# Attention and three-way maxout on one core: a fourth sum bank, reordered sums and splits, and pairs of batches run to and fro

## The chip, the core and the metric

The kernel runs on one core of a Trainium2 chip. A core has a matrix engine (TensorE, in the profile PE, with its weight loads as PEld), VectorE (DVE), ScalarE (ACT), GpSimd (POOL) and a queue that issues transfers (SyncE, SP). Matrix products go into PSUM, eight banks of 512 fp32 columns per partition; VectorE and ScalarE read them from there; everything else lies in SBUF or, through transfers, in HBM. The metric is the device time of one execution in microseconds (us), as the median of several runs. Lower is better.

## The reference

```python
scores = scale * np.matmul(q, k.transpose(0, 1, 3, 2)) - np.log(S)
attn = 1.0 / (1.0 + np.exp(-scores))
x = np.matmul(attn, v)                 # then laid out as (B * S, H * D)
h = np.maximum(np.maximum(x @ w1, x @ w2), x @ w3)
return (h @ w_out).astype(np.float32)
```

There are 8 batches, 12 heads, 448 positions and 64 columns a head, so `x` is 3584 x 768, and the four weights are 768 x 768. The weights reach the kernel as 64-bit numbers, and it turns them into fp32 itself.

## The kernel before

It has two phases. **Attention** runs 24 rounds (8 batches by 3 groups of four heads). A round computes scores (line L267, and the last 64 positions of both pairs of heads at L279), has ACT take the sigmoid (L258), and multiplies by v (L287, L296); the sums are copied out of PSUM by VectorE (L316) and stored to `x_dram`. In the background, two blocks a round, raw weights are decoded (two operations on ACT, L173 and L174, four on VectorE, L175 to L184). The generator `decoding` holds their order `todo`: the 12 blocks of stage 0 stay in SBUF, the 36 of later stages are stored to `w_dram` and fetched back when needed.

**Products** computes all four matrix products in 4 stages: stages 0 to 2 give one third of the rows of `h` each and take the maximum over the three weights (q = 0, 1, 2); stage 3 is the product with `w_out`, where q counts thirds of the output's rows. A stage visits 4 pairs of batches, so there are 16 visits (numbered 0 to 15 here), each with three passes q. A visit multiplies 2 x 2 blocks by a scheme with 7 block products instead of 8: `PRODUCTS` lists which sum of weight blocks meets which sum of x blocks, and which PSUM bank takes the result. The sums of blocks are made by POOL, for x (`x_load`, L231, four subtractions of 128x1344) and for weights (`w_combine`, L134). Each operand is split into a high part (a cast on ACT, L361 for x, L145 for weights) and the rest (a subtraction on VectorE, L362 for x, L146 for weights), and a product is three terms over three k-blocks: 9 matmuls of 448 columns (L370).

After product k, VectorE and ACT read the banks. With p1 = the first product, copied by ACT (L426): `u2` = second + p1 (L429), `u3` = second + fourth + p1 (L432), and four results m22, m11, m21, m12 are put together by `put` (L403 for a first or only value, L405, L408 and L409 where a maximum is taken). For stages 0 to 2 the results go to `h_dram`, for stage 3 to the output.

Every engine runs its instructions in the order in which the code records them (`pin`), and a transfer waits in SP's queue behind those recorded before. At the start of a visit the next visit's x blocks are fetched (`x_load`), and during q = 2 they are split, one name after each product. Weights of the next stage are fetched and split around the last visit and the first visit of a stage (`w_load`, `w_split`): q = 0's in the last visit, q = 1's and q = 2's in the first. The blocks of x, their parts and the weights' parts have one buffer each, so a fetch waits until the former content has been read.

Of the kernel before, what the change touches and what calls it, by code (L numbers as in the profile page):

```python
# [38 lines left out]
def attention_then_maxout(  # L39
# [58 lines left out]
    m_p = pool(ctx, "m", 1)  # L98
    ps_av = pool(ctx, "ps_av", 1, space=PSUM)
# [48 lines left out]
    def decoding(dec_p):  # L148
# [64 lines left out]


    def x_load(src, p):


        r = {}
        for row in range(2):
            for th in range(2):  # L220
                name = f"b{row + 1}{th + 1}"
                r[name] = xs_p.tile([P, HALF, S], F32, name=f"xs_{name}")
                t = (2 * p + th) * S
                pin(nc.sync.dma_start(out=r[name], in_=src[row][:, :, t : t + S]))
# [3 lines left out]
        for out, in0, in1 in (  # L228
            ("t1", "b12", "b11"), ("t2", "b22", "t1"), ("t3", "b22", "b12"), ("t4", "b21", "t2"),
        ):  # L230
            pin(nc.gpsimd.tensor_tensor(out=r[out], in0=r[in0], in1=r[in1], op=ALU.subtract))  # L231
        return r


    def attention(stack):
# [68 lines left out]
        def load(n):  # L304
            if n < len(fours):
                b, f = fours[n]
                first = load_qk(b, 2 * f)
                vt = load_v(b, f)
                loads[n] = (first, load_qk(b, 2 * f + 1)), vt

        def finish(n, pss):
# [10 lines left out]
        before = xs = None  # L322
# [169 lines left out]
```

## Time and profile before

| | us |
|---|---|
| median of 3 runs | 1003.41 (1002.44 to 1004.03) |
| the profiled execution | 1008.24 |
| its span, first to last instruction | 1006.5 |
| PE busy | 924.3 (92% of the span) |
| VectorE busy | 599.9 |
| ScalarE busy | 413.9 |
| GpSimd busy | 257.4 |
| attention, up to the first product | 292.97 |

A busy share is a mean over phases: ScalarE is busy 205 of the first 293 us and little later. Matmuls overlap each other, so PE's busy time counts short waits only in part; a stretch of matmuls, from start to start, tells more.

### The profile page before, as it was taken

How to read it: one execution, taken by the hardware profiler on the slowest of the kernel's cores; microseconds unless marked ns; L12 is line 12 of the kernel's file. 1: busy time of each engine (PE TensorE's matmuls, PEld its weight loads, DVE VectorE, ACT ScalarE, POOL GpSimd, SP SyncE). 2: the span in 40 equal slices, each digit the busy share in tenths (PEclk: the TensorE clock that was granted, in tenths of full speed). 3: DMA queues.
4: the chain of work that ended last, by engine and by line, in shares of the span. 5: the costliest groups of instructions: out<-in, count | busy, mean ns of one | idle time of the engine just before them, and what ended most of it. 6: DMA issues, size and time to landing. Idle time of an engine off the chain costs nothing.

```text
span 1006.5 us, 12056 instructions
## 1 busy us (share of the span) xinstructions
PE 924.3 (92%) x4560; PEld 684.5 (68%) x4560; DVE 599.9 (60%) x794; ACT 413.9 (41%) x513; POOL 257.4 (26%) x116
## 2 busy tenths in 40 slices
PE   6999998999989999978799998879999969799998
PEld 2333333333348898867789897768889858699997
DVE  2656745644463765848884673888575658656262
ACT  5777676776770421414241330415042223324130
POOL 0110102200004044062604225351404352431400
PEclk9999999999998999999799999889999979899999
DMA  5767778777842304131412404140330514252421
GB/s 206 231 233 238 264 259 314 267 270 243 272 150 66 123 24 147 45 141 61 141 40 107 147 19 159 50 160 19 128 113 34 178 32 174 78 183 80 177 74 74
DMA packets 74043, 143.93 MB, mean 143 GB/s; under 512 B 6400, under 2 KB 58624, under 8 KB 73984
## 3 DMA queue, kind: packets, MB, share of 16 engines
q1 hardware_dynamic: 73984, 143.16, 41.4%
q8 instruction: 36, 0.59, 0.2%
q14 instruction: 23, 0.19, 0.1%
HBM read 103.02 MB, written 40.11 MB: 142 GB/s over the span
## 4 chain that ended last, share of the span: by engine, by line
PE 57%; DVE 25%; DMA 6%; issue 6%; ACT 3%; POOL 2%; SPq 1%; DVEq 0%; ACTq 0%; POOLq 0%
PE ps_y L370 35%; PE ps_av L287 9%; PE ps_s L267 9%; DVE xlo_t L362 8%; DVE xlo_b L362 5%; DMA xs_b<-x_dram 2%; DVE c L408 2%; PE ps_av L296 2%; DVE wlo_a L146 2%; DMA xs_b<-h_dram 2%; DVE u L429 2%; PE ps_s L279 1%; ACT a L258 1%; DVE wlo_s L146 1%; DMA qk<-qk 1%
## 5 line engine op out<-in xcount | busy, mean ns | idle before, releaser
L370 PE MATMUL ps_y<-xhi_t,wlo_s 128*128 128x448 f32 x432 | 165.0, 382 | 43.3 <-DVE u L429 43.3
L231 POOL TENSOR_TENSOR xs_t<-xs_b,xs_b 128x1344 f32<-128x1344 f32 x16 | 49.6, 3103 | 558.6 <-DMA xs_b<-x_dram 435.2
L258 ACT ACTIVATE a<-ps_s,bias_s 128x896 f32<-128x896 f32 x168 | 158.2, 1005 | 83.5 <-PE ps_s L279 44.6
L370 PE MATMUL ps_y<-xhi_t,whi_s 128*128 128x448 f32 x432 | 161.9, 375 | 0.0
L370 PE MATMUL ps_y<-xlo_t,whi_s 128*128 128x448 f32 x432 | 161.8, 375 | 0.1
L267 PE MATMUL ps_s<-qk 64*128 64x448 f32 x576 | 125.2, 568 | 11.5 <-DMA qk<-qk 8.2
L370 PEld LDWEIGHTS ps_y<-xhi_t,wlo_s 128*128 128x128 f32 x432 | 83.2, 193 | 62.0 <-DVE u L429 49.1
L287 PE MATMUL ps_av<-a,v 128*64 128x448 f32 x576 | 119.9, 552 | 2.6 <-DVE m L316 2.6
L426 ACT COPY p<-ps_y 128x448 f32<-128x448 f32 x48 | 25.6, 533 | 230.5 <-PE ps_y L370 227.7
L267 PEld LDWEIGHTS ps_s<-qk 64*128 64x128 f32 x576 | 52.8, 190 | 81.1 <-issue 55.0
L370 PE MATMUL ps_y<-xhi_b,wlo_a 128*128 128x448 f32 x288 | 107.6, 373 | 0.0
L183 DVE CUSTOM_DVE_ANT_0 wb<-wraw,wb 128x768 uint16<-128x768 uint16 x48 | 32.9, 685 | 124.9 <-ACT wraw L174 124.1
L370 PE MATMUL ps_y<-xlo_b,whi_a 128*128 128x448 f32 x288 | 106.9, 371 | 0.0
L370 PE MATMUL ps_y<-xhi_b,whi_a 128*128 128x448 f32 x288 | 106.4, 369 | 0.0
L231 POOL TENSOR_TENSOR xs_t<-xs_b,xs_t 128x1344 f32<-128x1344 f32 x32 | 100.3, 3135 | 9.6 <-DMA xs_b<-x_dram 7.6
L362 DVE TENSOR_TENSOR xlo_b<-xs_b,xhi_b 128x1344 fp32r<-128x1344 f32 x48 | 76.3, 1589 | 36.5 <-PE ps_y L370 19.8
L287 PEld LDWEIGHTS ps_av<-a,v 128*64 128x64 f32 x576 | 37.5, 138 | 80.8 <-issue 62.3
L370 PEld LDWEIGHTS ps_y<-xhi_t,whi_s 128*128 128x128 f32 x432 | 83.8, 194 | 7.2
L370 PEld LDWEIGHTS ps_y<-xlo_t,whi_s 128*128 128x128 f32 x432 | 83.5, 193 | 6.9 <-DVE xlo_t L362 0.5
L401 ACT COPY m<-ps_y 128x448 f32<-128x448 f32 x24 | 12.8, 533 | 160.8 <-PE ps_y L370 160.8
L362 DVE TENSOR_TENSOR xlo_t<-xs_t,xhi_t 128x1344 fp32r<-128x1344 f32 x48 | 75.6, 1601 | 0.0
L370 PE MATMUL ps_y<-xhi_t,wlo_a 128*128 128x448 f32 x144 | 55.3, 384 | 21.2 <-DVE u L432 21.2
(58 smaller groups left out, 1449.4 us busy)
## 6 DMA issues: line engine op xcount, KB each, us to landing
xs_b<-x_dram SPq DMA_DIRECT2D x48, 672.0 KB, 6.7
qk<-qk SPq DMA_DIRECT2D x48, 448.0 KB, 4.5
wraw<-w SPq DMA_DIRECT2D x36, 384.0 KB, 6.2
v<-v SPq DMA_DIRECT2D x24, 448.0 KB, 3.4
x_dram<-m SPq DMA_DIRECT2D x48, 224.0 KB, 6.1
h_dram<-m SPq DMA_DIRECT2D x48, 224.0 KB, 1.9
xs_b<-h_dram SPq DMA_DIRECT2D x16, 672.0 KB, 7.5
outT<-m SPq DMA_DIRECT2D x48, 224.0 KB, 1.9
```

What stands on the lines that cost most here:

```text
L146: pin(nc.vector.tensor_tensor(out=lo, in0=r[name], in1=hi.bitcast(F32), op=ALU.subtract))
L183: pin(nc.vector.tensor_tensor(out=bits, in0=bits, in1=low, op=ALU.add))
L231: pin(nc.gpsimd.tensor_tensor(out=r[out], in0=r[in0], in1=r[in1], op=ALU.subtract))
L258: pin(nc.scalar.activation(out=a, in_=ps[:, :, :S], func=AF.Sigmoid, bias=bias_s, scale=scale))
L267: pin(nc.tensor.matmul(ps[:, e, :S], t[r, S + c * P : S + (c + 1) * P], t[r, :S], start=True, stop=True,))
L287: pin(nc.tensor.matmul(ps[e * D : (e + 1) * D, :S], vt[:, (g * C + c) * 2 + e], a[:, e], start=c == 0, stop=False,))
L296: pin(nc.tensor.matmul(ps[e * D : (e + 1) * D, :S], vt[r, 4 * C + e], a[r, e], start=False, stop=True,))
L362: pin(nc.vector.tensor_tensor(out=lo, in0=r[name], in1=hi.bitcast(F32), op=ALU.subtract))
L370: pin(nc.tensor.matmul(ps[:, :S], wt[:, k * P : (k + 1) * P], xt[:, k], start=first and n == 0, stop=n == len(terms) - 1, skip_group_check ...
L408: pin(nc.vector.tensor_tensor(out=c, in0=y, in1=add, op=ALU.add))
L426: pin(nc.scalar.copy(out=p1, in_=ps[0][:, :S]))
L429: pin(nc.vector.tensor_tensor(out=u2, in0=ps[1][:, :S], in1=p1, op=ALU.add))
```

## The change

The fourth product of `PRODUCTS` (s3 with t3) becomes the third and gets a bank of its own, and `u3` is now made from that bank and `u2`. The result m21 adds `u3` to a product that stands alone. Banks 0 and 1 keep two buffers, 2 and 3 have one, and line numbers move (products now L389, `u2` L481, `u3` L484, x splits L250, weight splits L148).

```diff
 PRODUCTS = (
     ("a11", "b11", 0),
     ("s2", "t2", 1),
+    ("s3", "t3", 3),
     ("s1", "t1", 2),
-    ("s3", "t3", 1),
...
-                first = ps[bank] is None
+                here = n, q, k
+                first = k < 4 or bank == 1
                 if first:
-                    ps[bank] = ps_y.tile([P, 512], F32, name=f"ps_y{bank}")
+                    ps[bank] = ps_y.tile(
+                        [P, 512], F32, name=f"ps_y{bank}", bufs=2 if bank < 2 else 1
+                    )
...
+                elif k == 2:
+                    u3 = c_p.tile([P, S], F32, name="u3", bufs=1)
+                    pin(nc.vector.tensor_tensor(out=u3, in0=ps[3][:, :S], in1=u2, op=ALU.add))
                 elif k == 3:
-                    u3 = c_p.tile([P, S], F32, name="u3", bufs=1)
-                    pin(nc.vector.tensor_tensor(out=u3, in0=ps[1][:, :S], in1=p1, op=ALU.add))
                     put("22", ps[2], u3)
...
-                    put("21", ps[1], p1)
+                    put("21", ps[1], u3)
```

Casts and splits are set by tables: after product k of pass q of visit n, `his` names an x cast, `los` an x split, `ws` weight splits, `w_loads` a fetch of weights. Stage 1 visits the pairs backwards, so the x of visit 3 serves visit 4, and that of visit 7 visit 8.

```diff
+    visits = [(st, p) for st in range(STAGES) for p in (pairs[::-1] if st == 1 else pairs)]
...
+    for n in range(1, done):
+        (st0, p0), (st, p) = visits[n - 1], visits[n]
+        if st != st0:
+            if st < LAST:
+                when = [[(n - 1, 1, k // 2) for k in range(7)],
+                        [(n - 1, 2, 2 + k // 2) for k in range(7)],
+                        [(n, 0, 3 + k // 2) for k in range(6)] + [(n, 1, 0)]]
+            else:
+                when = [[(n - 1, 1, k // 2) for k in range(7)],
+                        [(n - 1, 2, 5)] * 2 + [(n, 0, 1)] * 2 + [(n, 0, 4)] * 2 + [(n, 0, 5)],
+                        [(n, 1, 3 + k // 2) for k in range(7)]]
...
+            w_loads[n - 2, 0, 0] = st, 0
+            w_loads[when[0][-1]] = st, 1
+            w_loads[when[1][-1]] = st, 2
+        if (st == LAST, p) != (st0 == LAST, p0):
+            for k, (_, name, _) in enumerate(PRODUCTS):
+                his[n - 1, 2, k] = name
+            keys = [(n - 1, 2, k) for k in range(1, 5)] + [(n, 0, k) for k in (0, 2, 3)]
+            for key, (_, name, _) in zip(keys, PRODUCTS):
+                los[key] = name
...
+    for _, name, _ in PRODUCTS[2:4]:
+        x_lo(*x_hi(name, xs))
+    for k in (1, 2, 3):
+        his[0, 0, k - 1] = los[0, 0, k] = PRODUCTS[k + 3][1]
```

In attention, the first call of the generator only issues loads; 8 blocks of later stages follow each 4 of stage 0, and one weight split of stage 0 goes behind each; the buffer `wd` of a decoded block is single; q and k are loaded ahead of v; the first pair is fetched in 12 pieces, one a round from round 10 on, instead of 4 blocks in round 12; the first two x operands are cast and split while the last matmuls of attention run (their pool `xo` now lies beside attention's).

```diff
-            todo += first[4 * q : 4 * q + 4] + later[2 * q : 2 * q + 2]
-        todo += later[6:]
+            todo += first[4 * q : 4 * q + 4] + later[8 * q : 8 * q + 8]
+        todo += later[24:]
...
+            if k == 0:
+                yield
...
-                out = dec_p.tile([P, HP], F32, name="wd", bufs=2)
+                out = dec_p.tile([P, HP], F32, name="wd", bufs=1)
                 decode(raws[k], out)
                 pin(nc.sync.dma_start(out=w_dram[st, q][:, n], in_=out))
-                if ready and k > 16:
-                    for name, _, _ in PRODUCTS:
-                        w_split(ready[0], name, ready[1], nc.vector.tensor_copy)
-                    ready = None
+                if splits:
+                    w_split(*splits.pop(0), nc.vector.tensor_copy)
...
+            else:
+                for _, name, _ in PRODUCTS[:2]:
+                    x_lo(*x_hi(name, xs))
...
-            if n == len(fours) // 2:
-                xs = x_load(x_dram, 0)
+            part = n - 10
+            if 0 <= part < 4 * HALF:
+                x_block(xs, x_dram, 0, part // HALF // 2, part // HALF % 2, part % HALF)
+                if part == 4 * HALF - 1:
+                    x_combine(xs)
```

Three places in the order of instructions carry the prediction. The first is VectorE's queue around the end of visit 0 and the start of visit 1, from m11 of q = 2 to the first results of q = 0 (`xlo` are splits, `u2`, `u3`, `m` and `c` the sums). Before:

```order
L405 TENSOR_TENSOR m11_2512<-ps_y0_2618,m11_2512 128x448
L362 TENSOR_TENSOR xlo_b21_2695<-xs_b21_2445,xhi_b21_2694 128x1344
L408 TENSOR_TENSOR c_2707<-ps_y1_2634,p1_2628 128x448
L409 TENSOR_TENSOR m21_2523<-c_2707,m21_2523 128x448
L362 TENSOR_TENSOR xlo_t4_2712<-xs_t4_2451,xhi_t4_2711 128x1344
L408 TENSOR_TENSOR c_2724<-ps_y2_2650,u2_2644 128x448
L409 TENSOR_TENSOR m12_2534<-c_2724,m12_2534 128x448
L362 TENSOR_TENSOR xlo_b22_2729<-xs_b22_2447,xhi_b22_2728 128x1344
L429 TENSOR_TENSOR u2_2769<-ps_y1_2759,p1_2757 128x448
L432 TENSOR_TENSOR u3_2790<-ps_y1_2759,p1_2757 128x448
```

The same stretch after the change:

```order
L454 TENSOR_TENSOR m11_2518<-ps_y0_2633,m11_2518 128x448
L250 TENSOR_TENSOR xlo_t1_2695<-xs_t1_2442,xhi_t1_2694 128x1344
L457 TENSOR_TENSOR c_2723<-ps_y1_2713,u3_2674 128x448
L458 TENSOR_TENSOR m21_2536<-c_2723,m21_2536 128x448
L457 TENSOR_TENSOR c_2739<-ps_y2_2680,u2_2658 128x448
L458 TENSOR_TENSOR m12_2547<-c_2739,m12_2547 128x448
L250 TENSOR_TENSOR xlo_b21_2710<-xs_b21_2438,xhi_b21_2709 128x1344
L481 TENSOR_TENSOR u2_2784<-ps_y1_2774,p1_2771 128x448
L484 TENSOR_TENSOR u3_2796<-ps_y3_2786,u2_2784 128x448
L250 TENSOR_TENSOR xlo_t4_2728<-xs_t4_2444,xhi_t4_2727 128x1344
L452 TENSOR_TENSOR m22_2809<-ps_y2_2799,u3_2796 128x448
L250 TENSOR_TENSOR xlo_b22_2744<-xs_b22_2440,xhi_b22_2743 128x1344
```

Three splits (b21, t4, b22) have moved from between the last sums of q = 2 into q = 0 of the next visit, each behind that product's sum.

The second place is VectorE's queue from the last decoded block of attention on. Before:

```order
L184 SCALAR_TENSOR_TENSOR wd_2365<-wa_2366,wb_2367 128x384
L362 TENSOR_TENSOR xlo_b11_2408<-xs_b11_1371,xhi_b11_2407 128x1344
L362 TENSOR_TENSOR xlo_t2_2412<-xs_t2_1380,xhi_t2_2411 128x1344
L316 COPY m11_2415<-ps_av0_2375 128x448
L316 COPY m12_2418<-ps_av1_2376 128x448
L362 TENSOR_TENSOR xlo_t1_2422<-xs_t1_1379,xhi_t1_2421 128x1344
L362 TENSOR_TENSOR xlo_t3_2426<-xs_b12_1373,xhi_t3_2425 128x1344
L362 TENSOR_TENSOR xlo_b21_2430<-xs_b21_1375,xhi_b21_2429 128x1344
L362 TENSOR_TENSOR xlo_t4_2434<-xs_t4_1381,xhi_t4_2433 128x1344
L362 TENSOR_TENSOR xlo_b22_2438<-xs_b22_1377,xhi_b22_2437 128x1344
L429 TENSOR_TENSOR u2_2478<-ps_y1_2468,p1_2466 128x448
```

After the change:

```order
L250 TENSOR_TENSOR xlo_t2_2399<-xs_t2_2210,xhi_t2_2398 128x1344
L250 TENSOR_TENSOR xlo_t3_2427<-xs_b12_1441,xhi_t3_2426 128x1344
L250 TENSOR_TENSOR xlo_t1_2431<-xs_t1_2209,xhi_t1_2430 128x1344
L481 TENSOR_TENSOR u2_2474<-ps_y1_2464,p1_2459 128x448
L250 TENSOR_TENSOR xlo_b21_2462<-xs_b21_1742,xhi_b21_2461 128x1344
L484 TENSOR_TENSOR u3_2490<-ps_y3_2480,u2_2474 128x448
L250 TENSOR_TENSOR xlo_t4_2477<-xs_t4_2211,xhi_t4_2476 128x1344
L452 TENSOR_TENSOR m22_2506<-ps_y2_2496,u3_2490 128x448
L250 TENSOR_TENSOR xlo_b22_2493<-xs_b22_2023,xhi_b22_2492 128x1344
L334 COPY c_2520<-ps_av0_2386 128x448
L334 COPY c_2523<-ps_av1_2387 128x448
```

`u2` now stands behind four splits instead of seven and two copies; the copies are behind the third result.

The third place is POOL's queue in visits 11 and 12 of the changed kernel, where stage 3 begins (`xs` sums belong to x, `ws` to weights):

```order
L231 TENSOR_TENSOR xs_t4_5913<-xs_b21_5907,xs_t2_5912 128x1344
L136 TENSOR_TENSOR ws_s1_6088<-ws_a21_6082,ws_a22_6083 128x384
L136 TENSOR_TENSOR ws_s2_6089<-ws_s1_6088,ws_a11_6080 128x384
L136 TENSOR_TENSOR ws_a21_6082<-ws_a11_6080,ws_a21_6082 128x384
L136 TENSOR_TENSOR ws_s4_6090<-ws_a12_6081,ws_s2_6089 128x384
L231 TENSOR_TENSOR xs_t1_6259<-xs_b12_6253,xs_b11_6251 128x1344
L231 TENSOR_TENSOR xs_t2_6260<-xs_b22_6257,xs_t1_6259 128x1344
L231 TENSOR_TENSOR xs_b12_6253<-xs_b22_6257,xs_b12_6253 128x1344
L231 TENSOR_TENSOR xs_t4_6261<-xs_b21_6255,xs_t2_6260 128x1344
L136 TENSOR_TENSOR ws_s1_6371<-ws_a21_6365,ws_a22_6366 128x384
L136 TENSOR_TENSOR ws_s2_6372<-ws_s1_6371,ws_a11_6363 128x384
```

and in the kernel before, at the same place:

```order
L231 TENSOR_TENSOR xs_t4_5910<-xs_b21_5904,xs_t2_5909 128x1344
L134 TENSOR_TENSOR ws_s1_5923<-ws_a21_5917,ws_a22_5918 128x384
L134 TENSOR_TENSOR ws_s2_5924<-ws_s1_5923,ws_a11_5915 128x384
L134 TENSOR_TENSOR ws_a21_5917<-ws_a11_5915,ws_a21_5917 128x384
L134 TENSOR_TENSOR ws_s4_5925<-ws_a12_5916,ws_s2_5924 128x384
L134 TENSOR_TENSOR ws_s1_6128<-ws_a21_6122,ws_a22_6123 128x384
L134 TENSOR_TENSOR ws_s2_6129<-ws_s1_6128,ws_a11_6120 128x384
```

The sums for q = 0 of stage 3 are gone from this place (they are made in visit 10 now); those for q = 2 stay behind the pair's subtractions in both.

More of the change, by code (lines that the diff above doesn't have):

```diff
@@ L98, in attention_then_maxout @@
     m_p = pool(ctx, "m", 1)
+    xo_p = [pool(ctx, "xo", 1)]
     ps_av = pool(ctx, "ps_av", 1, space=PSUM)
@@ L187, in decode @@
             ))
-        stage, ready = None, None
+        stage, splits = None, []
         for k, (st, q, n) in enumerate(todo):
@@ L202, in decoding, with x_block, x_combine @@
                     w_combine(stage)
-                    ready = q, stage
+                    splits = [(q, name, stage) for name, _, _ in PRODUCTS]
             else:
-                out = dec_p.tile([P, HP], F32, name="wd", bufs=2)
+                out = dec_p.tile([P, HP], F32, name="wd", bufs=1)
                 decode(raws[k], out)
                 pin(nc.sync.dma_start(out=w_dram[st, q][:, n], in_=out))
-                if ready and k > 16:
-                    for name, _, _ in PRODUCTS:
-                        w_split(ready[0], name, ready[1], nc.vector.tensor_copy)
-                    ready = None
+                if splits:
+                    w_split(*splits.pop(0), nc.vector.tensor_copy)
             yield
[L215 to L224, printed above, removed]
+        assert not splits
+    def x_block(r, src, p, row, th, k=None):
+        name = f"b{row + 1}{th + 1}"
+        if name not in r:
+            r[name] = xs_p.tile([P, HALF, S], F32, name=f"xs_{name}")
+        ks = slice(0, HALF) if k is None else slice(k, k + 1)
+        t = (2 * p + th) * S
+        pin(nc.sync.dma_start(out=r[name][:, ks], in_=src[row][:, ks, t : t + S]))
+    def x_combine(r):
         for name in ("t1", "t2", "t4"):
@@ L231, in x_load, with x_hi, x_lo @@
             pin(nc.gpsimd.tensor_tensor(out=r[out], in0=r[in0], in1=r[in1], op=ALU.subtract))
-        return r
+    def x_load(src, p):
+        r = {}
+        for row in range(2):
+            for th in range(2):
+                x_block(r, src, p, row, th)
+        x_combine(r)
+        return r
+    FIRST = [x for _, x, _ in PRODUCTS[:2]]
+    def x_hi(name, r):
+        hi = xo_p[name not in FIRST].tile([P, HALF, S], F32R, name=f"xhi_{name}")
+        lo = xo_p[name not in FIRST].tile([P, HALF, S], F32R, name=f"xlo_{name}")
+        pin(nc.scalar.copy(out=hi, in_=r[name]))
+        return name, r[name], hi, lo
+    def x_lo(name, x, hi, lo):
+        pin(nc.vector.tensor_tensor(out=lo, in0=x, in1=hi.bitcast(F32), op=ALU.subtract))
+        x_ops[name] = hi, lo
     def attention(stack):
@@ L306, in load, with finish @@
                 b, f = fours[n]
[L307 to L311, printed above, removed]
+                ts = load_qk(b, 2 * f), load_qk(b, 2 * f + 1)
+                loads[n] = ts, load_v(b, f)
+        def finish(n, pss, pool=m_p, names=("m11", "m12")):
             b, f = fours[n]
@@ L321, in attention @@
         load(0)
-        before = xs = None
+        before, xs = None, {}
         for n in range(len(fours) + 1):
```

74 lines of the change are left out of this document (33 added, 41 removed).

## The prediction

> **What bounds the kernel now.** I start with the chain of work that ended last, by engine, to see which engine sets the end.
>
> ```profile
> PE 57%; DVE 25%; DMA 6%; issue 6%; ACT 3%; POOL 2%; SPq 1%; DVEq 0%; ACTq 0%; POOLq 0%
> ```
>
> PE carries the chain, and VectorE a quarter of it: PE has too much to do to be fed late, and VectorE feeds it late. To see where, I cut the busy time of the product line (L370) into stretches: attention, visit 0, visits 1 and 2, then by turns the two visits around a change of stage and two quiet ones, at last visits 13 and 14, and visit 15. The columns are the stretch, its length, PE's busy time (matmuls), the granted clock, the DMA share and GB/s.
>
> ```profile
> 0.00:292.97 292.97, 0.00 (x1) 0.99 0.73 248
> 292.97:339.47 46.50, 41.53 (x189) 0.93 0.24 75
> 339.47:420.04 80.57, 77.68 (x379) 1.00 0.26 92
> 420.04:521.21 101.17, 84.93 (x379) 0.92 0.28 96
> 521.21:601.77 80.56, 77.70 (x379) 1.00 0.26 92
> 601.77:701.98 100.21, 84.44 (x379) 0.91 0.28 97
> 701.98:782.94 80.96, 78.41 (x379) 1.00 0.26 91
> 782.94:886.68 103.74, 85.16 (x380) 0.90 0.33 114
> 886.68:964.55 77.87, 77.14 (x380) 1.00 0.40 142
> 964.55:1006.47 41.92, 38.46 (x190) 1.00 0.21 78
> 886.68:912.21 25.53, 25.53 (x127) 1.00 0.51 182
> ```
>
> The last row is a stretch without a wait: 14 products (126 matmuls) in 25.53 us, so a product takes 1.824 us and a visit of 21 at least 38.3 us. That is the floor that this change can't lower. Each stretch minus its floor is what the change can win: 8.2 us in visit 0; 4.0, 4.0 and 4.4 in the three quiet pairs (12.3); 24.6, 23.6 and 27.1 around the changes of stage (75.4); 1.3 in visits 13 and 14. Visit 15 has 3.6 us, the drain of the last block, which both kernels have.
>
> What ends a wait in a quiet visit is seen in VectorE's and PE's rows in order of time (start, length, operation; in brackets the idle time before it and who ended it):
>
> ```profile
> 344.05 1.55 DVE L362 TENSOR_TENSOR xlo_b<-xs_b,xhi_b 128x1344 fp32r<-128x1344 f32 x1
> 345.52 0.62 DVE L429 TENSOR_TENSOR u<-ps_y,p 128x448 f32<-128x448 f32 x1
> ...
> 346.20 0.47 PE L370 MATMUL ps_y<-xhi_t,wlo_s 128*128 128x448 f32 x1 [1.10 <-DVE u L429]
> ```
>
> The product s3·t3 wants the bank that `u2` is still to read, and `u2` stands behind a split.
>
> In attention the length of a round (from one L279 to the next) shows the losses; the fifth stretch belongs to a later argument:
>
> ```profile
> 8.76:25.34 16.58, 13.35 (x66) 4.46 (x68) 5.65 (x12) 10.35 (x15) 0.00 (x0) 0.90 0.44 168
> 25.34:36.73 11.39, 11.39 (x69) 4.21 (x65) 5.67 (x10) 8.38 (x11) 4.17 (x4) 1.00 0.70 232
> 48.12:60.45 12.33, 11.46 (x69) 4.21 (x64) 8.06 (x18) 8.48 (x11) 0.00 (x0) 1.00 0.64 215
> 164.84:181.59 16.75, 13.10 (x68) 4.78 (x64) 12.99 (x10) 8.59 (x11) 11.50 (x4) 0.90 0.89 337
> 479.20:482.50 3.30, 3.30 (x11) 2.92 (x10) 0.59 (x2) 0.00 (x0) 0.00 (x0) 0.50 1.03 388
> ```
>
> A round is 11.39 us with PE busy throughout (second row). The first is 5.2 us longer, one with a whole batch of 14 weight-split operations 0.94, the one in which the first pair is loaded 5.4.
>
> **The change, part by part.** The lengths that I use, by form from the product phase (count | busy, mean ns):
>
> ```profile
> L362 DVE TENSOR_TENSOR xlo_b<-xs_b,xhi_b 128x1344 fp32r<-128x1344 f32 x48 | 76.3, 1589 | 36.5 <-PE ps_y L370 19.8 <-ACT xhi_b L361 16.7
> L409 DVE TENSOR_TENSOR m<-c,m 128x448 f32<-128x448 f32 x72 | 54.6, 758 | 2.5
> ...
> L361 ACT CAST xhi_t<-xs_t 128x1344 fp32r<-128x1344 f32 x47 | 62.1, 1321 | 16.6 <-PE ps_y L370 15.3
> ```
>
> *Quiet visits.* s3·t3 now writes bank 3, and s1·t1 bank 2, so nothing of the third and fourth product waits for `u2`. The earliest new wait is the seventh product, which needs `m22`'s sum from bank 2. I walked VectorE's queue from the second product of q = 2 at 0.62 us a sum (the `u2` above), about 1.5 a split (they overlap by some 0.08) and 0.25 from a product's end to its reader. The four splits in q = 2 leave VectorE 2 us behind PE at the visit's end, and it catches up in the next q = 0, where only three splits are left. There `b22`'s split, the last, starts 8.3 us into the visit and ends at 9.9; the seventh product, which reads it, begins at 10.9. One microsecond of slack: no wait. ACT's seven casts at 1.32 fit one to a product. So -12.3, and -1.3 in visits 13 and 14 (the bound on the other side is 0).
>
> *Visit 0.* In the kernel before, seven splits and two copies stand ahead of the first `u2`; now four splits, two of them made while attention's last matmuls run, and the copies follow the fifth product. Same walk, no wait: -8.2 (bounds -8.2 and -4, if the casts of the pool behind attention start late).
>
> *Attention.* Loading 4 raw blocks without decoding the first lets ACT go on with sigmoids, where it stood until the block landed:
>
> ```profile
> 12.73 0.55 ACT L173 ACTIVATE wa<-wraw 128x384 f32<-128x384 f32 x1 [2.84 <-DMA wraw<-w]
> ```
>
> PE's stall behind it and the half clock after it go: -5.0 (bounds -5.2 and 0). One weight split per decoded block instead of seven in a row: three times -0.94, -2.8. The pair's 12 pieces, one a round, take 224 KB of transfer each instead of 2.7 MB at once, and q's and k's tiles no longer queue behind them. But the four subtractions on POOL stay, and they hold VectorE:
>
> ```profile
> 173.12 3.36 POOL L231 TENSOR_TENSOR xs_t<-xs_b,xs_t 128x1344 f32<-128x1344 f32 x1 [0.53 <-DMA xs_b<-x_dram]
> ...
> 173.51 3.18 DVE L175 TENSOR_SCALAR wb<-wraw 128x384 uint32<-128x384 uint32 x1
> ...
> 361.04 3.11 POOL L231 TENSOR_TENSOR xs_t<-xs_b,xs_t 128x1344 f32<-128x1344 f32 x1
> ...
> 362.40 2.23 DVE L409 TENSOR_TENSOR m<-c,m 128x448 f32<-128x448 f32 x1
> ```
>
> An operation of 0.35 us (0.62 in the second pair) that reads and writes SBUF alone lasts until POOL's ends; so while POOL works, VectorE does one such operation per 3.1 us, whereas sums from PSUM go on. One of the four now falls beside weight splits (about 1.7 us late for the copies out of PSUM), three beside decoding (0.4): -5.4 + 2.1 = -3.3 (bounds -5.4 and 0). The Trainium skill ("SBUF — State Buffer", section "Who interferes with whom") says the same: VectorE and GpSimd share a port pair as an exclusive lock, taken also by VectorE operations with two SBUF inputs, and issue order decides who blocks. The trace agrees (2.23 us where 0.62 is usual). Read strictly, it speaks against this change, which moves splits into the stretch where POOL starts; that is the second rival below.
>
> *Changes of stage.* The chain before is POOL, then ACT, then VectorE, then PE:
>
> ```profile
> 447.75 2.07 DVE L146 TENSOR_TENSOR wlo_s<-ws_s,whi_s 128x384 fp32r<-128x384 f32 x2 [8.02 <-ACT whi_s L145]
> ...
> 450.41 0.74 PE L370 MATMUL ps_y<-xhi_t,wlo_a 128*128 128x448 f32 x1 [6.71 <-DVE u L432]
> ```
>
> Weights are now fetched a visit earlier, so their sums on POOL stand ahead of the pair's, and at two of three changes the pair stays (stage 1 runs back), with 7 casts, 7 splits, 4 loads and 4 subtractions less each. Visits 3 and 7 then have no POOL work beside their splits: nothing is late. What comes back, by the lock:
> - Visits 4 and 8: q = 2's weights split under the next pair's subtractions; VectorE reaches `m12`'s sum of q = 0 about 2 us after the next q wants bank 2. +2 each.
> - Visit 11: q = 0's weights split from 15 us into the visit, just when POOL runs three subtractions (15 to 24 us, since `b22` can only be fetched after its split). Two splits cost 3 us each, and two more; `m22` of q = 1 is ready at 27.0, PE wants it at 23.7: +3.3, and half clock after it.
> - Visit 12: POOL sums q = 2's weights only behind the pair's subtractions: +1.6 to 4, say 2.5.
>
> A wait brings half clock. The row 479.20:482.50 above shows 0.50 for 3.3 us, and what preceded it was short:
>
> ```profile
> 478.85 0.47 PE L370 MATMUL ps_y<-xhi_t,wlo_s 128*128 128x448 f32 x1 [1.82 <-DVE u L429]
> ```
>
> So I add 2 us to visit 11's wait. The Trainium skill ("TensorE: Matmul & The Clock Gate", Part 1) lets the clock fall only after an idle window of about 3.4 us; the trace has it after 1.82. By the page the sum would be 2 us less. In all 2 + 2 + 5.3 + 2.5 = 11.8 come back: -75.4 + 11.8 = -63.6 (bounds -75.4 and -40).
>
> *Sum.* -5.0 - 2.8 - 3.3 - 8.2 - 12.3 - 1.3 - 63.6 = -96.5. The profiled execution took 1008.24 us (span 1006.47), which gives 911.7; the runs shown have a median of 1003.41, 0.48% less, and at that ratio it is **907 us**.
>
> **Rivals.**
>
> 1. *Everything is hidden*, the locks too: -110.4 in all, 894 us at the same ratio. For it: VectorE's slack in most places; against it: the rows of the lock.
>
> 2. *The lock meets `b22`'s split in quiet visits.* POOL's first subtraction starts when `b12` has landed:
>
> ```profile
> xs_b<-x_dram SPq DMA_DIRECT2D x48, 672.0 KB, 6.7
> ...
> w_dram<-wd SPq DMA_DIRECT2D x36, 192.0 KB, 4.2
> ```
>
> With the fetch behind `m12`'s store, 2.9 us into the visit, that is about 9.6; the split starts at 8.3. In stage 3 VectorE has no maxima, the fetch starts 1.4 earlier, and the two meet. Where POOL is first, the split ends some 2.7 us late, with 1.7 of half clock: 4.4 a visit, so 916 us if visits 13 and 14 are hit, 942 if all eight are. By the Trainium skill's rule on issue order (same page and section) each of these is a toss-up; no run here shows it yet.
>
> 3. *The fourth bank doesn't do it*: the wait moves from the fourth product to the seventh, since VectorE still has the same splits to do. The quiet visits keep their 13.6 us: 921. Against it: the slack of 1 us and more at the seventh product.
>
> 4. *Changes of stage keep a wait of 8 us in each of visits 4, 8, 11 and 12*, because each weight split pays 3.1: 32 instead of 11.8, 927 us.
>
> 5. *Slower than before:* the decoded block has one buffer `wd` now. The next block's last operation must wait until the last store has landed. Blocks follow each other every 5.7 us (two to a round of 11.39) and VectorE can run some 2 us late before PE feels it; so a landing of over 7.7 us, 48 times, makes the store the pace of attention. To lose the 96 us again takes 2 us a block more, a landing near 9.7. The row has a median of 4.2, so I give it little.
>
> **How the numbers follow.** Chances: forecast as worked out (900 to 914) 0.43; all hidden 0.14; rivals 2 to 4, between 914 and 932, 0.28; several of them together, above 932 but below before, 0.11; slower than before by rival 5 or something unseen 0.03; the last 0.01 for no change. The range 894 to 932 takes in the forecast, the first rival and those that add up to 25 us; what is left out is more than one of them at once, and the fifth. A measurement of this kernel tells 0.2% from no change; faster by more than that 0.96, within it 0.01, slower 0.03.
>
> **What would show it.** In the profile after: quiet visits of 38.3 us, with no PE idle time put down to `u2`; the first L279 round near 11.5 and no round of 16.75; PE's first product right behind attention and no gap in visit 0; waits on PE of more than 1 us only in visits 4, 8, 11 and 12, beside POOL's subtractions, with weight splits of 2 to 3 us there; 56 subtractions of pairs on POOL where there were 64, four less for each kept pair. I am wrong if quiet visits show a wait at the seventh product, if attention's rounds lengthen to 12 or more, or if VectorE's splits run under POOL in every visit.

## The result and the profile after

The changed kernel takes **918.96 us** (median of 4 runs, 908.96 to 923.52), the kernel before 1003.72 beside it: a ratio of 0.9114 (95% interval 0.9028 to 0.92). Measured again with more runs, it was 922.05 us (6 runs, 917.87 to 929.2) against 1004.65, ratio 0.9181 (0.9147 to 0.9215). Both ratios are of mean times, and the first leaves out the run of 923.52 us, which counts as slow. The prediction was 907, with a range of 894 to 932. What needs an explanation beside the gain is the spread: 11 runs of the kernel before beside the second measurement lie within 0.9%, the changed kernel's ten runs between 909 and 929 us, and the one with the first profile (908.96 us, span 907.2) is the fastest of them.

The chain of work that ended last, by engine, in that profile:

```profile
PE 88%; DVE 5%; issue 2%; DMA 2%; ACT 2%; POOL 1%; SPq 0%; DVEq 0%; POOLq 0%; ACTq 0%
```

PE has 88% of the chain instead of 57%, VectorE 5% instead of 25%. The matmuls of the products (now L389) in the stretches of the prediction: visit 0, visits 1 and 2, then by turns around a change of stage and quiet (visits 11 and 12 apart), 13 and 14, 15, and a piece of visit 11. Columns: stretch, length, PE's busy time (matmuls), granted clock, DMA share, GB/s.

```profile
281.67:321.47 39.80, 38.67 (x189) 1.00 0.30 93
321.47:398.08 76.61, 76.61 (x379) 1.00 0.31 107
398.08:475.24 77.16, 76.87 (x379) 1.00 0.24 81
475.24:551.85 76.61, 76.61 (x379) 1.00 0.32 107
551.85:628.46 76.61, 76.61 (x379) 1.00 0.24 81
628.46:705.07 76.61, 76.61 (x380) 1.00 0.32 107
705.07:749.11 44.04, 40.37 (x191) 0.96 0.31 102
749.11:788.65 39.54, 39.22 (x190) 1.00 0.47 160
788.65:865.26 76.61, 76.61 (x379) 1.00 0.42 145
865.26:907.18 41.92, 38.46 (x190) 1.00 0.21 77
733.24:736.65 3.41, 3.41 (x11) 0.50 0.40 140
```

Two visits at the floor are 76.61 us, and there length and busy time agree: no wait is left. The first product comes at 281.67 instead of 292.97. Losses, against 38.3 us a visit, stand in visit 0 (1.5), visits 3 and 4 (0.5), 11 (5.7, with 3.41 us of half clock: the granted clock of 0.50 in the last row) and 12 (1.2). The waits of visits 0 and 11, in PE's rows in order of time (start, length, operation; in brackets idle time and who ended it):

```profile
294.21 0.47 PE L389 MATMUL ps_y<-xlo_b,whi_s 128*128 128x448 f32 x1 [1.12 <-DVE xlo_b L250]
...
732.61 0.47 PE L389 MATMUL ps_y<-xhi_b,wlo_s 128*128 128x448 f32 x1 [3.67 <-DVE c L457]
```

And what VectorE and POOL did ahead of them, in the same view of these two engines:

```profile
288.71 4.03 POOL L231 TENSOR_TENSOR xs_t<-xs_b,xs_b 128x1344 f32<-128x1344 f32 x1 [18.56 <-DMA xs_b<-x_dram]
290.23 3.92 DVE L250 TENSOR_TENSOR xlo_b<-xs_b,xhi_b 128x1344 fp32r<-128x1344 f32 x1
...
722.89 3.43 POOL L231 TENSOR_TENSOR xs_b<-xs_b,xs_b 128x1344 f32<-128x1344 f32 x1
723.28 3.45 DVE L148 TENSOR_TENSOR wlo_s<-ws_s,whi_s 128x384 fp32r<-128x384 f32 x1
```

A split of x that takes 1.55 us elsewhere takes 3.92, a weight split of 0.55 takes 3.45: both begin while a subtraction of POOL runs and end somewhat less than their own usual length after it (288.71 + 4.03 is 292.7 and 290.23 + 3.92 is 294.1, 1.4 later; 726.3 and 726.7 are 0.4 apart). By these rows the split's own work comes after POOL's. I call this the lock. It is the one that the prediction took from the kernel before, here in `b22`'s split too, where the prediction had seen a microsecond of slack.

In attention, two rounds (first matmul of L298 to the next), the first one and the one with POOL's first subtraction:

```profile
9.17:20.80 11.63, 11.63 (x66) 1.00 0.56 214
191.62:204.14 12.52, 11.45 (x68) 1.00 0.86 291
```

In the kernel before, the first was 16.58 us and the one where the pair was loaded 16.75. The single buffer `wd` of the fifth rival shows in the view of waits (waiter, releaser: total us, times, longest), and is too small to reach PE:

```profile
DVE wd L186 <- DMA w_dram<-wd: 8.8, 9, 2.6
```

### The profile page after: what moved, and what is told of

Read it like the earlier page. It is cut to its first block, busy times and chain, and to the rows that moved or that the text cites. A ratio compares the mean times of both kernels' runs of the same rounds, so it can differ in the third digit from the quotient of the medians.

```text
span 907.2 us, 12118 instructions
## 1 busy us (share of the span) xinstructions
PE 892.6 (98%) x4560; PEld 670.8 (74%) x4560; DVE 568.9 (63%) x780; ACT 394.3 (43%) x499; POOL 233.1 (26%) x108
## 4 chain that ended last, share of the span: by engine, by line
PE 88%; DVE 5%; issue 2%; DMA 2%; ACT 2%; POOL 1%; SPq 0%; DVEq 0%; POOLq 0%; ACTq 0%
PE ps_y L389 62%; PE ps_s L286 12%; PE ps_av L306 11%; PE ps_av L315 2%; PE ps_s L298 2%; DMA xs_b<-h_dram 1%; DVE wlo_a L148 1%; DVE wlo_s L148 1%; ACT a L277 1%; DVE xlo_b L250 1%; DVE xlo_t L250 0%; DVE wd L186 0%; DVE wb L181 0%; DMA qk<-qk 0%; POOL xs_t L231 0%
## 5 line engine op out<-in xcount | busy, mean ns | idle before, releaser
L389 PE MATMUL ps_y<-xhi_t,wlo_s 128*128 128x448 f32 x432 | 158.1, 366 | 0.6 <-DVE wlo_s L148 0.3
L389 PE MATMUL ps_y<-xhi_t,whi_s 128*128 128x448 f32 x432 | 157.8, 365 | 0.0
L389 PE MATMUL ps_y<-xlo_t,whi_s 128*128 128x448 f32 x432 | 157.8, 365 | 0.0
L231 POOL TENSOR_TENSOR xs_t<-xs_b,xs_b 128x1344 f32<-128x1344 f32 x14 | 46.7, 3335 | 266.6 <-DMA xs_b<-x_dram 184.9
L231 POOL TENSOR_TENSOR xs_t<-xs_b,xs_t 128x1344 f32<-128x1344 f32 x28 | 90.1, 3218 | 93.2 <-DMA xs_b<-x_dram 85.5
L389 PE MATMUL ps_y<-xhi_b,wlo_a 128*128 128x448 f32 x288 | 105.5, 366 | 0.0
L389 PE MATMUL ps_y<-xlo_b,whi_a 128*128 128x448 f32 x288 | 105.4, 366 | 0.0
L389 PE MATMUL ps_y<-xhi_b,whi_a 128*128 128x448 f32 x288 | 105.4, 366 | 0.0
L185 DVE CUSTOM_DVE_ANT_0 wb<-wraw,wb 128x768 uint16<-128x768 uint16 x48 | 27.9, 581 | 107.4 <-ACT wraw L176 106.5
L306 PEld LDWEIGHTS ps_av<-a,v 128*64 128x64 f32 x576 | 37.2, 136 | 77.1 <-issue 56.1
L389 PEld LDWEIGHTS ps_y<-xhi_t,wlo_s 128*128 128x128 f32 x432 | 81.1, 188 | 8.0 <-DVE m L452 0.8
L389 PEld LDWEIGHTS ps_y<-xhi_t,whi_s 128*128 128x128 f32 x432 | 81.1, 188 | 6.5
L389 PEld LDWEIGHTS ps_y<-xlo_t,whi_s 128*128 128x128 f32 x432 | 81.2, 188 | 6.5
L452 DVE TENSOR_TENSOR m<-ps_y,u 128x448 f32<-128x448 f32 x72 | 44.6, 621 | 58.6 <-PE ps_y L389 58.6
L481 DVE TENSOR_TENSOR u<-ps_y,p 128x448 f32<-128x448 f32 x48 | 29.9, 623 | 78.3 <-PE ps_y L389 69.8
L136 POOL TENSOR_TENSOR ws_s<-ws_a,ws_a 128x384 f32<-128x384 f32 x12 | 12.6, 1050 | 257.3 <-DVE ws_a L186 155.3
L250 DVE TENSOR_TENSOR xlo_b<-xs_b,xhi_b 128x1344 fp32r<-128x1344 f32 x42 | 67.5, 1607 | 0.0
```

Source lines behind the costliest of these rows:

```text
L185: pin(nc.vector.tensor_tensor(out=bits, in0=bits, in1=low, op=ALU.add))
L250: pin(nc.vector.tensor_tensor(out=lo, in0=x, in1=hi.bitcast(F32), op=ALU.subtract))
L306: pin(nc.tensor.matmul(ps[e * D : (e + 1) * D, :S], vt[:, (g * C + c) * 2 + e], a[:, e], start=c == 0, stop=False,))
L389: pin(nc.tensor.matmul(ps[:, :S], wt[:, k * P : (k + 1) * P], xt[:, k], start=first and n == 0, stop=n == len(terms) - 1, skip_group_check ...
L452: pin(nc.vector.tensor_tensor(out=m[name], in0=y, in1=add, op=ALU.add))
L481: pin(nc.vector.tensor_tensor(out=u2, in0=ps[1][:, :S], in1=p1, op=ALU.add))
```

## The experiments

All are edits of the changed kernel unless another is named. Of the runs quoted, the profile is of one execution, the time the median of all.

**1. The spread, and the lock.** Two theories for it: *lock*, a shift of under 1 us decides whether POOL's subtraction or VectorE's split starts first; *pace*, matmuls without any wait stand further apart in some executions (after visit 11's half clock the profile has 206.7 ns instead of 202.7 until 777 us). First the changed kernel once more, as it is (`again`):

> The changed kernel once more. Its profiled execution took 909 us, three others 917 to 923. Theory lock: in the slower executions POOL's first subtraction of a pair (L231) starts before VectorE's split of b22 (L250) in some quiet visits, the split takes 3 to 4 us instead of 1.55, and the seventh product of q = 0 waits 1 to 1.2 us, as in visit 0 of the 909 us execution; 4 to 8 such visits and their half clock make 8 to 14 us. Theory pace: no new wait; the matmuls' distance is 206.6 ns instead of 202.7 over several hundred us after visit 11's wait (1.9%, up to 4 us after visit 11, up to 12 us if it is there from the start). Median 917 to 921 by both.

922.05 us. In its profile (922.92 us, span 921.1) visits 4, 8, 9 and 10, and 14 (stretches as above):

```profile
435.78:480.17 44.39, 41.06 (x190) 0.92 0.30 101
595.08:638.98 43.90, 40.23 (x191) 0.96 0.31 102
638.98:717.10 78.12, 78.12 (x380) 1.00 0.31 105
839.56:879.23 39.67, 38.57 (x190) 1.00 0.41 140
```

Each theory has its rows. Visits 4 and 8 lose 6.1 and 5.6 us to waits of 3.3 and 3.7 and the half clock behind them, visit 14 loses 1.4 to `b22`'s split. Visits 9 and 10 have no wait at all (length and busy time agree, clock 1.00) and are 1.5 us longer than two visits at the floor: that is pace. I had looked for the locks in the quiet visits; they were mostly in visits 4 and 8. Of the 13.9 us between the two profiles 11 are in these two visits, 1.5 in visits 9 and 10, and 1.4 in visit 14. What decides in visit 4, first in the profile of the 909 us execution (VectorE's and POOL's rows; `wlo` is a weight split):

```profile
447.20 0.55 DVE L148 TENSOR_TENSOR wlo_s<-ws_s,whi_s 128x384 fp32r<-128x384 f32 x1
447.30 3.40 POOL L231 TENSOR_TENSOR xs_t<-xs_b,xs_b 128x1344 f32<-128x1344 f32 x1 [0.90 <-DMA xs_b<-x_dram]
```

then in this one:

```profile
446.43 3.39 POOL L231 TENSOR_TENSOR xs_t<-xs_b,xs_b 128x1344 f32<-128x1344 f32 x1 [0.44 <-DMA xs_b<-x_dram]
446.80 3.44 DVE L148 TENSOR_TENSOR wlo_s<-ws_s,whi_s 128x384 fp32r<-128x384 f32 x1
...
457.51 0.74 PE L389 MATMUL ps_y<-xhi_t,wlo_s 128*128 128x448 f32 x1 [3.33 <-DVE m L452]
```

In the first the fourth weight split starts 0.1 us before POOL and takes 0.55; in the second POOL is 0.4 us ahead and it takes 3.44. Those 3 us are the wait of 3.33, and half clock follows. The Trainium skill's rule on issue order ("SBUF — State Buffer", section "Who interferes with whom") is what these two pairs of rows show, with its size.

**2. Taking the lock away by order** (`b12_last`). `b12`, which POOL's first subtraction reads, is loaded last, behind `b22`, whose buffer is free only when its split is done:

```diff
-        for row in range(2):
-            for th in range(2):
-                x_block(r, src, p, row, th)
+        for row, th in ((0, 0), (1, 0), (1, 1), (0, 1)):
+            x_block(r, src, p, row, th)
```

> The block b12 of a pair is loaded last instead of second, so that all four subtractions of POOL stand behind the landing of b22 and thus behind VectorE's split of the old b22. Theory lock: no split of x beside POOL any more; visit 0 38.3 to 38.7 us instead of 39.8, every quiet visit 38.3 in every execution, visit 11 as before (44 us or somewhat more, since the weight splits there still stand beside POOL); 908 to 911 us, and a spread under 4 us. Theory pace: visit 0 gains 1.1 us, the spread stays at 909 to 922.

923.94 us (914.55 to 924.98): no gain. The profile is of an execution of 914.89 us; the four that took 923.9 to 925.0 have none, so what they lost is not known. In the profile visits 0, 4 and 8 came out as lock says, 38.4, 38.3 and 38.3, and no quiet visit is over 38.4. But visit 12 grew to 47.1 us. POOL's rows there, and PE's wait:

```profile
774.73 3.03 POOL L231 TENSOR_TENSOR xs_t<-xs_b,xs_t 128x1344 f32<-128x1344 f32 x1
777.72 0.98 POOL L136 TENSOR_TENSOR ws_s<-ws_a,ws_a 128x384 f32<-128x384 f32 x1
...
781.20 0.74 PE L388 MATMUL ps_y<-xhi_t,wlo_s 128*128 128x448 f32 x1 [5.69 <-DVE wlo_s L148]
```

The weights of q = 2 are combined on POOL behind the later subtractions, and PE waits 5.69 us for their split. I had not asked what stands behind the subtractions in POOL's queue.

**3. Visit 11** (`early_w`). Its seven weight splits are moved into q = 0, ahead of most subtractions, and the fetch of q = 1's weights moves with them:

```diff
-                when = [[(n - 1, 1, k // 2) for k in range(7)],
+                when = [[(n - 1, 0, k) for k in (1, 1, 2, 3, 4, 5, 6)],
```

> The seven weight splits of stage 3, q = 0 are made in q = 0 of visit 11, ahead of POOL's subtractions, instead of in q = 1, beside them. Theory lock: visit 11 38.3 to 39.5 us instead of 44.0 and no half clock there, visit 12 38.3 to 39; the best execution 902 us, the spread of 909 to 922 moves down by 7 but stays, since the quiet visits are as before. Theory pace: the half clock of visit 11 is gone, and with it the cause of the slow pace: the spread goes too, 902 to 905 us in nearly all executions. A third theory (visit 11 waits because ACT and VectorE have too much to do there, whoever is beside them): visit 11 keeps 3 to 5 us, moved to q = 0.

915.53 us (913.63 to 918.93), some 6.5 less than the changed kernel measured beside it. Visit 11 is at the floor, so its 5.7 us were the lock; the third theory falls. Six of the seven splits now take 0.55 us, and one still meets POOL (3.46) without a wait on PE. Visits 1 and 11 of this profile:

```profile
321.49:360.55 39.06, 39.06 (x191) 1.00 0.28 94
720.66:758.97 38.31, 38.31 (x191) 1.00 0.35 117
```

Visit 1 is slow without a wait, and not because of a half clock: the distance changed to 206.7 ns at 293.7 us, at visit 0's wait of 1.12 us, with the clock at 1.00. In the execution of experiment 1 the same wait of 1.13 us changed nothing. So theory pace was wrong in its cause. The spread is 5.3 us instead of 11.3, but did not go, and the best execution was 913.63 us and not the 902 of theory lock: visits 4 and 8 of this profile still take 43.5 and 44.7 us.

Both edits together (`both`):

> Both edits. Theory lock: 901 to 904 us, spread under 4 us, no product wait over 0.5 us but the drain, except perhaps in visit 12, where the weight splits of q = 2 stand beside POOL's last two subtractions (up to 3 us). Theory pace: 901 to 904 us too, since no half clock is left.

912.38 us (911.25 to 920.04). Visit 11 takes 39.2 us, but visit 12 49.7, by the queue of experiment 2 (a wait of 6.8 us), and so the expected 901 to 904 was not reached.

**4. A version without either loss** (`mixed`). Both edits, with the old order of loads in visits 11 and 12:

```diff
+        for row, th in ((0, 0), (1, 0), (1, 1), (0, 1)) if last else ((0, 0), (0, 1), (1, 0), (1, 1)):
...
-            xs = x_load(x_dram if nst < LAST else h_dram, np_)
+            xs = x_load(x_dram if nst < LAST else h_dram, np_, n not in (done - 5, done - 4))
```

> The earlier weight splits of visit 11 (as in early_w), and b12 loaded last in every visit but 11 and 12 (in these two the raw weights of the next q would be combined on POOL behind the later subtractions, which made the 5.7 and 6.8 us waits in visit 12 of b12_last and both). Theory lock: visit 0 38.4, visits 4, 8 and 11 38.3, visit 12 39.5, all others 38.3; with attention's 281 and the drain of 3.6 that is 900 to 903 us, in all executions (spread under 4 us), since no split of x or of weights is left that a shift of 1 us would put beside POOL, except in visits 11 and 12. Theory pace alone: no half clock and no wait over 1.1 us, so the short distance throughout, the same time; they part if waits stay below 1.1 us and the distance of 206.7 ns shows up all the same (then 905 to 911).

909.6 us (902.48 to 912.3), ratio 0.9041 (0.9008 to 0.9075). The profiled execution took 902.77, as worked out, and its clock is 1.00 throughout the products; visit 0, visits 11 and 12:

```profile
281.23:319.64 38.41, 38.41 (x189) 1.00 0.28 91
703.47:742.39 38.92, 38.58 (x191) 1.00 0.35 120
742.39:782.44 40.05, 38.69 (x190) 1.00 0.48 159
```

Four of six executions took 908.6 to 912.3, so the spread did not shrink to 4 us. To see what these lose, the same kernel was profiled twice more (`mixed_again`, `mixed_third`).

> The kernel of mixed once more: its executions fell into two groups, 902.5 and 908.5 to 912.3, all with a granted clock of 0.999 or 1.0, so no half clock parts them. Theory pace: in an execution of the second group the matmuls stand 206.7 ns apart from the first product on, until a wait sets them right (the ones at about 715 and 771 us in the profile of mixed): 2139 to 2420 matmuls by 4.0 ns, 8.6 to 9.7 us, and no new wait. Theory lock: the second group has new waits of VectorE's splits, 8 us in all, with 202.7 ns between. An execution of the first group tells nothing.

904.68 us (901.62 to 907.84), ratio 0.9016 (0.899 to 0.9042); the profile was of the shorter group (901.98).

> The kernel of mixed for the third time, one look: its two profiles so far were of the faster group (902.8 and 902.0 us), the other executions lie at 902 to 903 or at 906 to 912. Theory pace: if this one is of the slower group, its waits are those of the two profiles (0.3 us in visit 11, 0.4 to 1.4 us in visit 12) and the matmuls stand 206.7 ns apart over 250 to 450 us. Theory lock: new waits of 4 us or more in all. If it is of the faster group, the slower one stays without a profile.

906.95 us. The waits in the products are the old ones and the distance is 202.7 ns throughout; the loss is in attention, where neither theory had put it. VectorE's, POOL's and PE's rows:

```profile
258.87 3.04 POOL L231 TENSOR_TENSOR xs_t<-xs_b,xs_t 128x1344 f32<-128x1344 f32 x1 [65.79 <-DMA xs_b<-x_dram]
259.10 3.22 DVE L185 CUSTOM_DVE_ANT_0 wb<-wraw,wb 128x768 uint16<-128x768 uint16 x1 [2.78 <-ACT wraw L176]
262.35 3.27 DVE L186 SCALAR_TENSOR_TENSOR wd<-wa,wb 128x384 f32<-128x384 f32 x1
265.54 1.14 DVE L333 COPY m<-ps_av 128x448 f32<-128x448 f32 x2
...
266.21 0.97 PE L305 MATMUL ps_av<-a,v 128*64 128x448 f32 x4 [2.86 <-DVE m L333]
```

It is the lock again, now on decoding: the last three subtractions of the first pair start 2 us earlier than in the 902.77 us profile (there at 260.95), so that two decoding operations of 0.56 us, which ran ahead of POOL there, meet it and take 3.2 and 3.3. The copy from PSUM stands behind them, and PE waits 2.86 us, with half clock after it. That execution's mean clock is 0.998. The executions of 906 to 912 us with 0.999 or 1.0 have no such half clock; a distance of 206.7 ns over part of the products would fit their size, but none of them was profiled, so that stays open.

**5. The fourth bank alone undone** (`bank_undone`). Tables and everything else as changed:

```diff
-    ("s3", "t3", 3),
     ("s1", "t1", 2),
+    ("s3", "t3", 1),
...
-                first = k < 4 or bank == 1
+                first = bank not in ps
...
-                elif k == 2:
-                    pin(nc.vector.tensor_tensor(out=u3, in0=ps[3][:, :S], in1=u2, op=ALU.add))
...
+                    pin(nc.vector.tensor_tensor(out=u3, in0=ps[1][:, :S], in1=p1, op=ALU.add))
...
```

> The changed kernel with the order of products, the banks and the sum u3 of the kernel before (s1 t1 third, s3 t3 fourth and on the bank of u2); tables and all else as changed. Theory bank (the fourth bank wins the 2 us of each quiet visit): the wait for u2 comes back, 1 to 1.1 us in q = 2 of each visit with a pair to split and up to 2 us a visit, 12 to 25 us in all. Theory order (what wins them is that each split is now issued a product later, behind u2): u2 is on time in all quiet visits, they stay at 38.3, and the time is that of the changed kernel within its spread (910 to 923).

933.45 us (931.74 to 934.52), ratio 0.929 (0.9267 to 0.9314). Visits 1 and 2, visit 4, visit 8:

```profile
320.85:397.46 76.61, 76.61 (x380) 1.00 0.31 107
435.76:483.38 47.62, 40.47 (x191) 0.93 0.27 94
600.56:648.81 48.25, 41.70 (x191) 0.89 0.27 92
```

Visits 1, 2, 9 and 10 are at the floor without the bank, and no quiet visit waits for `u2`: theory order holds there. (Visits 5 and 6 are 39.06 each at 206.7 ns without a wait; visits 13 and 14 lose 1.5 and 1.4 to `b22`'s split.) The profile is 10.5 us longer than that of experiment 1, and 7.6 of them are in visits 4 and 8, where VectorE is late by the lock, and `u2` with it (waits of 7.2 and 6.6 us). The same edit in the version of experiment 4 (`mixed_bank`):

> The kernel of mixed, with order of products, banks and u3 as in the kernel before (as in bank_undone). Theory A (the fourth bank is worth something only where VectorE is several us late, and it was late in visits 4, 8 and 11 only because of POOL's subtractions): visits 4 and 8 38.3 us instead of 47.6 and 48.3, quiet visits 38.3, time within 3 us of mixed in the same pace (902 or 909 to 912). Theory B (the bank has a price of its own at the stage changes, where weight splits fill VectorE): visits 4 and 8 keep 42 us or more, 910 to 925.

912.55 us (912.29 to 914.89), against 904.68 with the bank beside it, and 909.6 with it in the earlier measurement. Neither theory: visits 4 and 8 fall to 39.3 and 39.1, but other visits grow, visit 2 to 40.0. POOL's, VectorE's and PE's rows in its q = 2:

```profile
385.42 3.50 POOL L231 TENSOR_TENSOR xs_t<-xs_b,xs_t 128x1344 f32<-128x1344 f32 x1
386.50 2.89 DVE L457 TENSOR_TENSOR m<-c,m 128x448 f32<-128x448 f32 x1
389.31 0.61 DVE L480 TENSOR_TENSOR u<-ps_y,p 128x448 f32<-128x448 f32 x1
...
389.98 0.47 PE L388 MATMUL ps_y<-xhi_t,wlo_s 128*128 128x448 f32 x1 [0.44 <-DVE u L480]
394.56 0.47 PE L388 MATMUL ps_y<-xhi_t,wlo_a 128*128 128x448 f32 x1 [0.66 <-DVE u L483]
```

The later subtractions now hold the maxima (0.62 us elsewhere, 2.89 here), and `u2` is late again. With the bank, in the profile of 901.98 us, the same maxima are held (2.82, 2.34 and 2.88 us), but no product waits and visit 2 is 38.31. The bank pays where VectorE is late, whatever made it late.

**6. The spread of the splits over q = 2 and the next q = 0, undone** (`split_q2`):

```diff
-            keys = [(n - 1, 2, k) for k in range(1, 5)] + [(n, 0, k) for k in (0, 2, 3)]
+            keys = [(n - 1, 2, k) for k in range(7)]
```

> The changed kernel with all seven splits of x on VectorE in q = 2, each issued right behind its product, as before the change (fourth bank and all else as changed). By the count of VectorE's work in q = 2: seven splits of 1.55 and sums of 5.6 us are 16.4 us against 12.8, so VectorE is 3.6 us late at the visit's end. Theory spread (this lateness must show as waits): 1 to 2 us in each of 12 visits, 12 to 24 us more. Theory slack (the fourth bank holds the sums' lateness, and b22 is read only 10.9 us into the next visit): quiet visits stay at 38.3. Theory lock for both: no split of x stands beside POOL's subtractions any more, so visit 0 of the first pair is as changed (39.8), and visits 1, 2, 14 never show a split of 3 to 4 us.

925.19 us (921.95 to 930.25). Visits 5 and 6, 11 and 12:

```profile
482.00:558.61 76.61, 76.61 (x380) 1.00 0.31 107
715.54:761.99 46.45, 41.16 (x190) 0.93 0.28 98
761.99:804.09 42.10, 39.12 (x190) 1.00 0.43 154
```

Theory slack holds: in quiet visits the spreading buys nothing. But `u2` is late there, behind the splits. Visit 5, the first matmul of the fourth product and `u2`:

```profile
487.47 0.37 PE L389 MATMUL ps_y<-xhi_t,wlo_s 128*128 128x448 f32 x1
...
488.55 0.62 DVE L481 TENSOR_TENSOR u<-ps_y,p 128x448 f32<-128x448 f32 x1
```

The product starts 1.7 us before `u2` ends and does not wait: it writes another bank than the one that `u2` reads. In experiment 5 it is the other way round: no fourth bank, but `u2` ends 0.9 us before the fourth product starts (visit 1). So each of the two edits takes the wait for `u2` away without the other. The spreading is worth about 4 us in visits 11 and 12, where pair and weights meet (88.6 us against 84.2 in experiment 1). In the medians the difference, 0.9219 against 0.9181, is not clear of the noise.

**7. Pairs run forwards in stage 1** (`forward`):

```diff
-    visits = [(st, p) for st in range(STAGES) for p in (pairs[::-1] if st == 1 else pairs)]
+    visits = [(st, p) for st in range(STAGES) for p in (pairs)]
```

> The changed kernel with stage 1 running the pairs 0 to 3 as the others do, so that a new pair is loaded, subtracted and split in visits 3 and 7 too. Theory lock: the weight splits of q = 0 stand beside POOL's subtractions in visits 3 and 7 as they do in visit 11, 5 to 7 us each, and the splits of x at the ends of visits 3 and 7 stand beside weight splits on VectorE, so 10 to 20 us more than the changed kernel on the same chip. Rival (to and fro only saves loads that are hidden anyway): same time within the spread, and visits 3 and 7 at 38.3.

942.19 us (938.52 to 951.4), 20 more than the changed kernel (its ratio of 0.9396 against 0.9181). The profile is of the longest execution, 951.4. Visits 3 and 4, 7 and 8:

```profile
403.73:497.36 93.63, 82.17 (x380) 0.95 0.28 96
575.48:669.96 94.48, 83.73 (x380) 0.91 0.28 95
```

The rival falls: 93.6 and 94.5 us against 82.7 and 82.2 in the profile of experiment 1. The kernel before took 101.2 and 100.2, so in these profiles about 23 of the 36 us that the four visits won hang on the pair that stays, and some 13 on the other edits.

**8. The first pair in one piece** (`one_load`), in the version of experiment 4:

```diff
-            part = n - 10
-            if 0 <= part < 4 * HALF:
...
+            if n == 12:
+                xs = x_load(x_dram, 0, False)
```

> The kernel of mixed, with the first pair loaded whole in round 12 of attention instead of in 12 pieces over rounds 10 to 21 (q and k are still loaded ahead of v). If the pieces win what the prediction counts, the round of 12 takes 16.7 us as in the kernel before instead of 11.4, the later round with POOL's subtraction 11.4 instead of 12.5, and the first product comes at 285 us instead of 281.7. Rival (the loss of that round came from v ahead of q and k in the queue, not from the size of the load): the first product at 281 to 282 us.

910.84 us (909.35 to 912.74). The round of the load:

```profile
167.80:187.15 19.35, 13.76 (x69) 0.82 0.48 158
```

It takes 19.35 us, and the first product comes at 287.14 instead of 281.23 (in mixed): the pieces are worth 5.9 us, more than the 3.3 counted. The order of q, k and v does not explain the loss. Why the round is 2.6 us longer than in the kernel before was not found.

## Why the prediction was right, and where not

The terms, from the stretches of the three profiles (us; before to after; predicted is the prediction's sum). The sums are the differences of the spans, 1006.47 to 907.2 and to 921.1:

| term | predicted | first profile | experiment 1 |
|---|---|---|---|
| attention | -11.1 | -11.3 | -11.9 |
| visit 0 | -8.2 | -6.7 | -6.7 |
| six quiet visits | -12.3 | -12.3 | -10.8 |
| visits 13 and 14 | -1.3 | -1.3 | +0.1 |
| changes of stage | -63.6 | -67.8 | -56.1 |
| sum | -96.5 | -99.3 | -85.3 |

That the sum lies within 3 us of the first profile is in part luck: this is the shortest of ten executions, and it escaped most of what the sum had put into visits 4 and 8. Against the profile of experiment 1, which is near the median, the sum is 11 us too large.

- *Attention* came to the forecast. Within it the pair's term was 0.6 too small (3.9 net, since 1.1 and 0.3 came back in two rounds instead of 2.1). One round is 12.52 us, which the prediction had named as a sign of being wrong, though its own 1.7 for that round gives 13.1. What I did not see is that the 2.1 is a toss: in the last profile of experiment 4 it is a wait of 2.86 and half clock. The new first round and the single weight splits were not undone alone.
- *Visit 0*: the step "no wait" failed. `b22`'s split met POOL, 3.92 instead of 1.55 us, and PE waited 1.1 us, in every profile of a kernel with this order of loads (1.7 without the fourth bank).
- *Quiet visits*: the size is right, the reason only half. I gave it to the fourth bank, and the bank is enough (experiment 6); but issuing each split a product later, behind `u2`, is enough too (experiment 5 has 76.61 without the bank). In the changed kernel, which has both, `u2` is 0.9 us early, so the bank is not needed there. The third rival falls, and so does the second for most visits: `b22`'s split met POOL in one of these eight visits in experiment 1 (visit 14, in stage 3 as foreseen), and cost 1.4 there instead of 4.4: the split was 2.6 us late as foreseen, but the slack took more than a microsecond of that, the wait was 1.1, and it brought no half clock.
- *Changes of stage*: visit 11 was predicted at 5.3 and took 5.7, by the rows predicted; experiment 3 removes it. Visit 12: 1.2 instead of 2.5 (in the first profile about half of it is the distance of 206.7 ns, in experiment 1 it is a wait of 0.9). Visits 4 and 8, **+2 each**, were the mis-sized terms: 0.5 and 0 in one execution, 6.1 and 5.6 in the other. I worked out one delay for a thing that has two outcomes, and gave it no half clock. With such places in visits 4, 8 and 14 and in attention one execution of ten came to 909 us, and the median lies between the forecast and the fourth rival (8 us in each of visits 4, 8, 11 and 12), which had the mechanism and the place, but too much in visit 12. Of what was won, experiment 7 shows the share of the pair that stays; visits 11 and 12, where none stays, went from 103.7 to 84 us all the same. That this is the earlier fetch of the weights is argued from the order and was not undone alone.
- *The step from the sum to the median* (0.48% down, as in the kernel before) had the wrong sign: the profile of the changed kernel is 10 us below its median. The sum itself, 911.7, is 2.7 off that profile.
- *All hidden* fell with the locks. *Slower than before* did not occur: VectorE waited for `wd`'s store nine times, 2.6 us at most. The buffer was not tried apart. This rival also counted 48 stores, where its row has 36; losing 96 us would take 2.7 us a store, not 2.

## What to carry to other kernels

For each VectorE operation that reads and writes only SBUF, ask whether a POOL operation can start before it: if the order hangs on under 1 us, forecast two times, not their mean, and make the order certain by what a load must wait for. Before a resource is given the credit for a wait that went, undo it alone, and then the other candidate alone: here the bank and the later issue of the splits were each enough in quiet visits, and the bank paid only where VectorE was late. What is moved later on a queue delays everything behind it there, as the weights' sums in visit 12.

## What the runs showed of the hardware

- Matmuls of 448 columns without a wait stand 202.7 or 206.7 ns apart, at a granted clock of 1.00 in both; a visit is then 38.30 or 39.06 us. The distance changes mostly at a wait of 0.3 us or more (in the profile of experiment 8 also near 415 us, without one), and the same wait of 1.12 us in visit 0 changed it in one execution and not in another. What decides was not found.
- Half clock came in pieces of 3.41, 6.83 or 10.24 us. Of the 12 waits between 2.8 and 3.7 us in the profiles after the change 11 had it in or behind them, one of 3.41 had not, and none of up to 2.24 had, while the kernel before has it behind 1.82 us. The Trainium skill ("TensorE: Matmul & The Clock Gate", Part 1) gives a window of 3413 ns, which the pieces match, but a wait shorter than a window was enough.
